# The order of GpSimd's mask and of the loads in the recurrence of a linear-attention and mixture-of-experts kernel

## The chip, the cores and the metric

The kernel runs on one core of one Trainium2 chip. The metric is device time in microseconds (us); six runs of the kernel before gave a median of 430.74 us, between 429.99 and 431.18. Engines are written as in the profile: PE is TensorE, PEld its weight loads, DVE is VectorE, ACT is ScalarE, POOL is GpSimd, SP is the sync engine, which here issues the DMAs.

## The reference

Two blocks follow one another. The first is a gated recurrence over time with one state of 48 x 48 for each of 4 x 8 heads:

```
state = np.zeros((B, H, D, D))            # B, H, S, D = 4, 8, 768, 48
for t in range(S):
    state = alpha[:, :, t, :, None] * state + einsum('bhd,bhe->bhde', k[:, :, t], v[:, :, t])
    y[:, :, t] = einsum('bhd,bhde->bhe', q[:, :, t], state)
```

Its output, as 3072 rows of 384, goes to a mixture of eight experts. Each row goes to the expert with the highest logit, and its result is scaled by that expert's softmax weight:

```
logits = x @ w_gate                       # (3072, 384) @ (384, 8)
expert_idx = argmax(logits)               # gate_w: its softmax probability
h = maximum(x[rows of e] @ w1[e], 0)      # w1[e]: 384 x 1024
y[rows of e] = h @ w2[e]                  # w2[e]: 1024 x 384
out = gate_w[:, None] * y
```

All inputs and the output are float32.

## The kernel before

**Chunks and pairs.** Time is cut into 24 chunks of 128 steps (six chunks for each of four batches). A chunk holds all eight heads. The main loop (L696) takes two chunks at a time, s = 2, 4, ..., 20, but the stages are staggered over several chunks: a pair works on the results of chunks s and s+1, the scores of s+2 and s+3, the transposes of s+3 and s+4, and the elementwise work of s+5 and s+6. The schedule is manual: the order of the calls in the text is the order of the instructions on each engine, and each engine executes its own in that order.

**One chunk.** `logs` (L324): ACT takes the logarithm of alpha. `cums` (L334): PE sums it over time with a triangular matrix into one PSUM bank named `cum`, of which there is one, and ACT makes two exponentials of it, `icp` (exp of the negative) and `cp`. `operands` (L356): POOL multiplies k by icp (L360) and q by cp (L362) into the tile kqb. `transposes` (L364): PE turns kqb by heads, ACT copies kT and DVE copies qT out of PSUM. `scores` (L376): PE multiplies kT and qT into sA and sB; DVE masks sA to dA; ACT copies sB to dB (L388), and POOL then zeroes the part of dB above the diagonal with an affine_select (L389). `weighs` (L420): PE multiplies dA and dB with v into y (L426). `reads` (L402): PE adds the query times the state U of the chunk before (L414). `products` and `state` (L440, L458): PE forms k times v, ACT or DVE takes it out of PSUM, POOL adds the old state and scales by the decay E. `rows`, `keep_rows`, `store_rows`: PE turns the results and forms the gate's logits, and SP stores 128 rows of x to DRAM.

**Ranks.** Every fourth chunk, `choose` (L489) picks the expert of each row on DVE, and POOL adds up the choices in `ohs` (L500). In the pair after, `rank_products` (L502) multiplies them on PE (L505, L506), behind the first `cums` of that pair, which gives each row its place in its expert's list.

**Loads.** alpha (a), k, q and v of a chunk are 192 KB each. `to_load` (L314) is one list of loads in the order of their issue; `more_loads(n)` (L320) issues the next n of it. Each pair issues 2, 2 and 5 of them, and SP's other DMAs stand between: `decay_out` after the first two, `store_rows(s-1)` after the second two, `decay_in` and `store_rows(s)` after the five. All are on SP's one queue. The tiles of a, k and q have five buffers each, v has six, so a load waits until the chunk five (or six) before is done with its buffer.

**The order on POOL in a pair** is: the state of s+1, the mask of dB for s+2, `operands(s+5)`, the state of s+2, small copies of logits for s and s+1, `operands(s+6)`, the mask of dB for s+3, some constants (`late_consts`, L176, iotas and casts in the first pairs), and the adds of ohs every second pair. On ACT it is: the copy of PSUM for the state, the logarithm of s+5, the copy of dB for s+2, the logarithm of s+6, the exponentials of s+5, the copy of kT for s+3, the copy of rows, the exponentials of s+6, kT for s+4, rows, and the copy of dB for s+3.

After the loop come the last two chunks and the routing (to about 152 us), then the eight experts with two layers of matmuls each (L968, L984), the gathers of rows and the stores of results by indirect DMAs on POOL.

Of the kernel before, what the change touches and what calls it, by code (L numbers as in the profile page):

```python
# [18 lines left out]
def kernel(  # L19
# [267 lines left out]
    with tc.tile_pool(name="ld", bufs=6) as ld, \  # L287
# [21 lines left out]
        def some_loads(names):  # L309
# [3 lines left out]

        to_load = [  # L314
            (n, x + d) for x in range(7, NT + 2)
            for n, d in ((("a", 1), ("k", 0), ("q", 0), ("v", -2)) * 2)[3 * (x > 7) :][:4]
        ]


        def more_loads(n):  # L320
            for _ in range(min(n, len(to_load))):
                load(*to_load.pop(0))
# [53 lines left out]
        def scores(s):  # L376
            d = st[s]
            sA = ps.tile([C, NP, C], F32, name="sA")
            sB = ps.tile([C, NP, C], F32, name="sB")
            for p in range(NP):  # L380
                for t, r in ((sA, 0), (sB, DP)):
                    nc.tensor.matmul(  # L382
                        t[:, p, :], lhsT=d["kT"][r : r + D, p, :], rhs=d["qT"][r : r + D, p, :], start=True, stop=True,
                    )
            d["dA"] = work.tile([C, NP, C], F32, name="dA")
            nc.vector.tensor_tensor(d["dA"][:], sA[:], cmask[:, None, :].to_broadcast([C, NP, C]), op=ALU.mult)
            d["dB"] = work.tile([C, NP, C], F32, name="dB")
            nc.scalar.copy(d["dB"][:], sB[:])  # L388
            nc.gpsimd.affine_select(  # L389
                d["dB"][:], d["dB"][:], compare_op=ALU.is_ge, fill=0.0,  # L390
                base=0, pattern=[[0, NP], [1, C]], channel_multiplier=-1,
            )
# [3 lines left out]
        def results_of(s):  # L396
            y = [ps.tile([C, 2, NP // 2, C], F32, name=f"y{h}") for h in range(2)]
            for i in range(2):
                st[s + i]["y"] = [t[:, i] for t in y]
            return y  # L400

        def reads(s, first=None):  # L402

            d = st[s]
            if s % NB == 0:
                return
            if first is None:
                first = s % 2 == 0 or s % NB == 1
            for n in range(NP // 2):
                for h in range(2):  # L410
                    p = n + h * (NP // 2)
                    for a in range(2):
                        r = a * DP
                        nc.tensor.matmul(  # L414
                            d["y"][h][at(p, a) : at(p, a) + DP, n, :],
                            lhsT=st[s - 1]["U"][r : r + D, p, :], rhs=d["qT"][r : r + D, p, :],
                            start=(n == 0 and first), stop=False, skip_group_check=True,
                        )

        def weighs(s, h, first=False):  # L420

            d = st[s]
            for n in range(NP // 2):
                p = n + h * (NP // 2)
                for a in range(2):
                    nc.tensor.matmul(  # L426
                        d["y"][h][at(p, a) : at(p, a) + DP, n, :],
                        lhsT=d["v"][:, 2 * p + a, :], rhs=d["d" + "AB"[a]][:, p, :],
                        start=(first and n == 0), stop=True, skip_group_check=True,
                    )  # L430

        def results_to(s, y, h):
            if h == 0:
                yT = work.tile([C, 2, 2, NP // 2, C], F32, name="yT", bufs=1)
                for i in range(2):
                    st[s + i]["yT"] = yT[:, :, i]
                st[s]["yTs"] = yT
            nc.vector.tensor_copy(st[s]["yTs"][:, h], y[h][:])

        def products(s):  # L440

            d = st[s]
            if s >= NT or s % NB + 1 == NB:
                return
            kv = ps.tile([C, NP, C], F32, name="s" + "BA"[s % 2])[:, :, :D]
            for p in range(NP):
                for i, r in enumerate((0, DP)):
                    nc.tensor.matmul(  # L448
                        kv[r : r + DP, p, :], lhsT=kqb[s % 4][:, 0, 2 * p + i, :], rhs=d["v"][:, 2 * p + i, :D],
                        start=True, stop=True,  # L450
                    )
            d["acc"] = work.tile([C, NP, D], F32, name="acc" + "BA"[s % 2], bufs=1)
            if s % 2:
                nc.vector.tensor_tensor(d["acc"][:], kv, st[s - 1]["U"][:, :, :D], op=ALU.add)
            else:
                nc.scalar.copy(d["acc"][:], kv)

        def state(s):  # L458
            d = st[s]
            if s >= NT or s % NB + 1 == NB:  # L460
                return
            if s % 2 == 0 and s % NB:
                nc.gpsimd.tensor_tensor(d["acc"][:], d["acc"][:], st[s - 1]["U"][:, :, :D], op=ALU.add)
            d["U"] = Ub[s % len(Ub)]
            nc.gpsimd.tensor_tensor(
                d["U"][:, :, :D], d["acc"][:], d["E"].unsqueeze(2).to_broadcast([C, NP, D]), op=ALU.mult,
            )
# [17 lines left out]
        def store_rows(s):  # L485
            r0 = s * C + (s >= NT // 2)
            nc.sync.dma_start(x_d[r0 : r0 + C, :], st[s]["xs"][:])
# [115 lines left out]
        def do(f, i, *a):  # L603
            if 0 <= i < NT:
                f(i, *a)
# [90 lines left out]
        for s in range(2, NT - 2, 2):  # L696
            more_loads(2)
            if s == 2:
                store_rows(0)
            do(decay_out, s + 4)  # L700
            more_loads(2)

            for _ in range(8 if s > NT - 8 else 0):
                next(parts, None)
            y = results_of(s)
            reads(s)
            reads(s + 1)

            weighs(s, 0)
            weighs(s, 1)  # L710
            products(s + 1)
            products(s + 2)
            weighs(s + 1, 0)
            results_to(s, y, 0)
            weighs(s + 1, 1)
            results_to(s, y, 1)
            state(s + 1)
            do(logs, s + 5)
            if hots:
                one_hots(hots.pop(0))  # L720
            scores(s + 2)
            do(logs, s + 6)
            do(cums, s + 5)
            ranks = y[0][:].rearrange("r i p t -> r (i p t)")
            ranked = [rank_products(g, ranks[:, : len(g) * E]) for g in groups_of if g[-1] == s - 1]
            counts = ranks[:, C : C + E]
            if s in (TE, ORD):

                nc.tensor.matmul(
                    counts, lhsT=ones_sq[:], rhs=ohs[:, s, :], start=True, stop=True, skip_group_check=True,  # L730
                )
            if s == ORD:
                early_slots(ranks[:, 2 * C : 2 * C + EB * NQ])
                fetch_lot(0)
            for r in ranked if s < ORD else ():
                slots_of(*r)
            transposes(s + 3)
            do(operands, s + 5)
            state(s + 2)
            rows(s)  # L740
            keep_rows(s)
            store_rows(s - 1)
            if s == ORD:
                for r in ranked:
                    slots_of(*r)
                key = standing(counts[0:1, :])
                one_hots(hots.pop(0))
                one_hots(hots.pop(0))
                route = rps.tile([C, Dm], F32, name="cum")
                tokens_of_slots(0, TE)  # L750
            do(cums, s + 6)
            do(transposes, s + 4)
            more_loads(5)
            do(decay_in, s + 4)
            rows(s + 1)
            keep_rows(s + 1)
            do(operands, s + 6)
            if s == TE:
                close_early(counts[0:1, 0:1])
            scores(s + 3)  # L760
            store_rows(s)
            if s == 2:

                nc.sync.dma_start(x_d[N // 2 : N // 2 + 1, :], zero_w[:])
            late_consts(s + 2)
            late_consts(s + 3)
            if s == ORD:
                choose(groups_of[-2])
            if hots:
                one_hots(hots.pop(0))  # L770
            for g in groups_of[:-2]:
                if g[-1] == s + 1:
                    choose(g)
            for _ in range(4 if s == NT - 8 else 0):
                next(parts, None)
# [25 lines left out]
        s = NT - 2  # L801
# [329 lines left out]
```

## Time and profile before

| | |
|---|---|
| median of six runs | 430.74 us (429.99 to 431.18) |
| the profiled execution | 432.11 us, span 430.2 us |
| PE busy | 421.1 us, 98% of the span |
| DVE, ACT, POOL busy | 140.6, 108.3, 140.3 us |
| mean granted PE clock | 0.994 |
| loop (pairs s = 2 to 20) | from 28.99 to 139.74 us |
| DMA | 59.43 MB, most of it in the first 140 us at about 200 GB/s; 114614 of 132576 packets under 512 B |

All times below are microseconds from the start of the span of this one execution. A line of an engine's order of time gives the start, the duration, the engine, the source line, the operation, the output and its inputs, and in brackets the idle time before it and what ended it. A line of the waits names who waited for whom: the total, how often, and the longest. The chain of work that ended last gives start and duration of each piece. A line with `SPq` is the issue of a DMA by the sync engine, not its transfer. The clock of PE is a share of full speed, as granted.

### The profile page before, as it was taken

What the parts mean: (1) busy time and instruction counts of PE and PEld (TensorE: products, weight loads), DVE (VectorE), ACT (ScalarE), POOL (GpSimd) and SP (SyncE); (2) the same over time, 40 slices, a digit from 0 to 9 for tenths busy, and PEclk for the clock granted to TensorE, in tenths of its full rate; (3) what the DMA queues carried; (4) which work ended last, traced back from release to release, by engine and by line L of the source; (5) the groups of instructions that cost most, each with busy time, mean ns of one, the idle gap of its engine ahead of it and who ended that gap; (6) DMA issues with size and microseconds to landing.
All of it is one profiled execution on the core that took longest, in us unless ns stands there. A gap on an engine that the chain in (4) does not pass through costs nothing.

```text
span 430.2 us, 7708 instructions
## 1 busy us (share of the span) xinstructions
PE 421.1 (98%) x2990; PEld 285.4 (66%) x2990; DVE 140.6 (33%) x414; ACT 108.3 (25%) x230; POOL 140.3 (33%) x254
## 2 busy tenths in 40 slices
PE   8999899999999999999999999999999999999995
PEld 6888788888889887555555555655655455565452
DVE  6434457575768834711012101201201101111100
ACT  4565455555542321111111111011111110011011
POOL 4395677576665150160160110024010010010011
PEclk9999899999999999999999999999999999999999
DMA  9999999999977242994542610724620050000000
GB/s 161 180 164 205 202 204 201 192 193 194 182 197 215 83 114 91 395 400 161 179 129 70 250 38 2 270 74 114 224 105 18 2 183 20 0 32 20 1 33 30
DMA packets 132576, 59.43 MB, mean 138 GB/s; under 512 B 114614, under 2 KB 127452, under 8 KB 132538
## 3 DMA queue, kind: packets, MB, share of 16 engines
q1 hardware_dynamic: 127720, 48.96, 45.1%
q0 software_dynamic: 3328, 9.94, 7.0%
q8 instruction: 24, 0.39, 0.4%
q10 hardware_dynamic: 1490, 0.02, 0.2%
q14 instruction: 14, 0.11, 0.1%
HBM read 49.32 MB, written 9.98 MB: 138 GB/s over the span
## 4 chain that ended last, share of the span: by engine, by line
PE 62%; issue 28%; POOL 5%; DMA 2%; SPq 1%; DVE 1%; POOLq 0%; ACT 0%; DVEq 0%
PE zp L984 16%; PE hp L968 14%; PE sA L382 5%; PE y L426 5%; PE tp L369 4%; PE xr L474 4%; PE cum L337 3%; POOL out_dram L990 3%; PE y L414 2%; PE xr L612 2%; PE xtp L960 1%; PE sB L448 1%; POOL xg L269 1%; PE hp L785 1%; DMA k_sb<-in_k_dram 1%
## 5 line engine op out<-in xcount | busy, mean ns | idle before, releaser
L984 PE MATMUL zp<-w,h_sb 128*128 128x384 f32 (+2 forms) x560 | 137.1, 487 | 0.0
L968 PE MATMUL hp<-xT,w 128*128 128x416 f32 (+3 forms) x384 | 125.1, 486 | 0.0
L984 PEld LDWEIGHTS zp<-w,h_sb 128*128 128x128 f32 (+2 forms) x560 | 73.6, 163 | 56.3 <-issue 14.8
L968 PEld LDWEIGHTS hp<-xT,w 128*128 128x128 f32 x384 | 71.8, 190 | 51.9 <-issue 37.8
L990 POOL DMA_INDIRECT out_dram<-zo,o_idx x26 | 25.8, 992 | 219.2 <-ACT zo L989 214.3
L973 DVE TENSOR_SCALAR h_sb<-hp 128x416 f32<-128x416 f32 (+3 forms) x32 | 17.8, 557 | 149.3 <-PE hp L968 149.3
L989 ACT ACTIVATE zo<-zp,gw 128x384 f32<-128x384 f32 x26 | 15.1, 580 | 123.7 <-PE zp L984 119.1
L975 ACT ACTIVATE h_sb<-hp 128x416 f32<-128x416 f32 (+3 forms) x32 | 15.7, 490 | 107.3 <-PE hp L968 107.3
L269 POOL DMA_INDIRECT xg<-x_rows,g_idx x26 | 25.1, 965 | 11.1 <-issue 6.4
L382 PE MATMUL sA<-qT,kT 48*128 48x128 f32 x192 | 28.2, 288 | 0.2 <-DVE qT L372 0.2
L382 PE MATMUL sB<-qT,kT 48*128 48x128 f32 x192 | 28.3, 288 | 0.0
L962 DVE COPY xT<-xtp 128x384 f32<-128x384 f32 (+3 forms) x29 | 13.0, 484 | 44.4 <-PE xtp L960 44.3
L426 PE MATMUL y<-dB,vb 128*64 128x128 f32 x192 | 25.3, 278 | 1.7 <-POOL dB L389 1.7
L360 POOL TENSOR_TENSOR kqb<-k_sb,icp 128x384 f32<-128x384 f32 x23 | 23.0, 1000 | 11.8 <-ACT icp L340 8.8
L382 PEld LDWEIGHTS sA<-qT,kT 48*128 48x128 f32 x192 | 23.6, 190 | 4.7 <-issue 2.1
L426 PE MATMUL y<-dA,vb 128*64 128x128 f32 x192 | 26.3, 277 | 0.0
L369 PE MATMUL tp<-ident,kqb 128*128 128x128 f32 x192 | 25.7, 277 | 0.2 <-POOL kqb L362 0.2
L369 PEld LDWEIGHTS tp<-ident,kqb 128*128 128x128 f32 x192 | 22.2, 143 | 5.3 <-issue 2.7
L474 PE MATMUL xr<-back,yT 128*128 128x104 f32 x192 | 25.1, 274 | 0.0
L474 PEld LDWEIGHTS xr<-back,yT 128*128 128x128 f32 x192 | 23.6, 192 | 0.8 <-ACT xs L481 0.2
L382 PEld LDWEIGHTS sB<-qT,kT 48*128 48x128 f32 x192 | 23.6, 190 | 0.0
L372 DVE COPY qT<-tp 128x512 f32<-128x512 f32 x24 | 16.5, 689 | 20.2 <-PE tp L369 20.1
(178 smaller groups left out, 436.9 us busy)
## 6 DMA issues: line engine op xcount, KB each, us to landing
w<-in_moe_w_dram SPq DMA_DIRECT2D x14, 1536.0 KB, 7.0
x_rows<-xs SPq DMA_DIRECT2D x24, 196.0 KB, 3.9
a_sb<-in_alpha_dram SPq DMA_DIRECT2D x24, 192.0 KB, 4.1
k_sb<-in_k_dram SPq DMA_DIRECT2D x24, 192.0 KB, 3.8
q_sb<-in_q_dram SPq DMA_DIRECT2D x24, 192.0 KB, 4.4
vb<-in_v_dram SPq DMA_DIRECT2D x24, 192.0 KB, 3.5
w<-in_moe_w_dram SPq DMA_DIRECT2D x12, 128.0 KB, 3.7
w<-in_moe_w_dram SPq DMA_DIRECT2D x8, 192.0 KB, 4.3
```

Source lines behind the costliest of these rows:

```text
L269: nc.gpsimd.indirect_dma_start(out=xg[:, j, :], out_offset=None, in_=x_d[: N + 1 if n else TE * C + 1, :], in_offset=bass.IndirectOffsetOn ...
L360: k.tensor_tensor(kq[:, 0, :, :D], d["k"][:], heads(d["icp"]), op=ALU.mult)
L369: nc.tensor.transpose(tp[:, p, :], pair(kqb[s % 4][:, i], p), ident[:])
L372: nc.vector.tensor_copy(d[n][:], tp[:])
L382: nc.tensor.matmul(t[:, p, :], lhsT=d["kT"][r : r + D, p, :], rhs=d["qT"][r : r + D, p, :], start=True, stop=True,)
L426: nc.tensor.matmul(d["y"][h][at(p, a) : at(p, a) + DP, n, :], lhsT=d["v"][:, 2 * p + a, :], rhs=d["d" + "AB"[a]][:, p, :], start=(first an ...
L474: nc.tensor.matmul(xr[:, p, :], lhsT=d["yT"][:, p // (NP // 2), p % (NP // 2), :], rhs=back[:, p, :], start=True, stop=True)
L968: nc.tensor.matmul(hp[:, c0:c1], lhsT=w1[:, a, f * C : (f + 1) * C], rhs=xT[:, a, c0:c1], start=(a == 0), stop=(a == DB - 1),)
L973: nc.vector.tensor_relu(h[:, f, c0:c1], hp[:, c0:c1])
L975: nc.scalar.activation(h[:, f, c0:c1], hp[:, c0:c1], AF.Relu)
L984: nc.tensor.matmul(zp[i * wd : (i + 1) * wd, :], lhsT=h[:, f, c : c + wd], rhs=w2[:, f, :], start=(f == 0), stop=(f == FB - 1), skip_group ...
L990: ins = nc.gpsimd.indirect_dma_start(out=out[:, :], out_offset=bass.IndirectOffsetOnAxis(ap=idx, axis=0), in_=zo[:], in_offset=None, bound ...
```

## The change

Two edits, both inside the recurrence. In every pair, `operands(s+6)` is issued after `scores(s+3)` in place of before it. Of the engines, only POOL has instructions of both: the mask of dB for chunk s+3 now stands ahead of the two multiplies of chunk s+6. (For s = TE = 16 the two small DVE instructions of `close_early` stay ahead of the scores.) In the pairs s = 18 and 20 there is no chunk s+6.

And the list of loads has another order from chunk 8 on. Before, the groups from x = 8 on were v(x-2), a(x+1), k(x), q(x); now they are k(x), v(x-2), a(x+1), q(x). The group of x = 7 (a8, k7, q7, v5) stays. The number of loads issued at each place stays.

```
         to_load = [
             (n, x + d) for x in range(7, NT + 2)
-            for n, d in ((("a", 1), ("k", 0), ("q", 0), ("v", -2)) * 2)[3 * (x > 7) :][:4]
+            for n, d in (
+                (("a", 1), ("k", 0), ("q", 0), ("v", -2)) if x == 7 else (("k", 0), ("v", -2), ("a", 1), ("q", 0))
+            )
         ]
...
             rows(s + 1)
             keep_rows(s + 1)
-            do(operands, s + 6)
             if s == TE:
                 close_early(counts[0:1, 0:1])
             scores(s + 3)
+            do(operands, s + 6)
             store_rows(s)
```

## The prediction

> **What bounds the kernel now.** The page first: TensorE (PE) is busy for nearly the whole span, so only PE's idle time and PE's slow time can be won.
>
> ```profile
> PE 421.1 (98%) x2990; PEld 285.4 (66%) x2990; DVE 140.6 (33%) x414; ACT 108.3 (25%) x230; POOL 140.3 (33%) x254
> ```
>
> Next, the view of who waited for whom, cut to PE. One wait stands out: the matmuls of `weighs` (L426) for the mask of dB that GpSimd (POOL) makes at L389. The weight loads of the same place add up to 1.96 us.
>
> ```profile
> PE y L426 <- POOL dB L389: 1.7, 1, 1.7
> ```
>
> Then the chain of work that ended last, around that wait. It names the cause: the load of k for chunk 8 lands 3.88 us after its issue, POOL's `operands(8)` waits for it, and the mask of chunk 5 stands behind both multiplies.
>
> ```profile
> 37.89 3.88 DMA k_sb<-in_k_dram
> ...
> 41.90 0.82 POOL kqb L360
> ...
> 42.86 0.99 POOL kqb L362
> 43.85 0.60 POOL dB L389
> ...
> 44.50 1.09 PE y L426 x14
> ```
>
> POOL's own order of time shows that it had nothing to do for 1.92 us before it:
>
> ```profile
> 39.66 0.32 POOL L482 COPY xs<-lgn 128x8 f32<-128x8 f32 x2
> 41.90 1.00 POOL L360 TENSOR_TENSOR kqb<-k_sb,icp 128x384 f32<-128x384 f32 x1 [1.92 <-DMA k_sb<-in_k_dram]
> ```
>
> Last, PE's busy time and granted clock in four neighbouring stretches of about 3.4 us (columns: length, busy, clock, DMA share, GB/s):
>
> ```profile
> 40.00:42.57 2.57, 2.57 (x68) 1.00 1.20 214
> 42.57:45.99 3.42, 1.71 (x24) 1.00 0.90 177
> 45.99:49.40 3.41, 3.41 (x22) 0.50 1.12 242
> 49.40:52.80 3.40, 3.40 (x29) 1.00 1.16 215
> ```
>
> The half-idle stretch is followed by 3.41 us at half clock, which costs 3.41/2 = 1.7 us. Elsewhere in the loop the clock reads 1.00. So the wait costs 2.08 us (42.42, where the next matmul was due, to 44.50) plus 1.7, about 3.8 us. The loop's pairs agree: the reads (L414) of pair s=4 start at 39.98 and those of s=6 at 54.46, 14.48 us, while pair s=10 (76.22 to 86.80), with the same matmuls but for two small ranking ones, takes 10.58.
>
> The DMA share is near 1 from 30 to 108 us: the sync queue (SP) is paced by its transfers, 0.4 to 1.1 us from one load's issue to the next.
>
> **The change, part by part.**
>
> *The mask moves ahead of `operands(s+6)`*, in eight pairs (s=2 to 16); nothing is added or removed. dB of chunk 5 is copied by ScalarE (ACT) from 40.12 to 40.71, so the mask (0.64) runs about 40.78 to 41.42, a microsecond before PE needs it at 42.42. The wait goes whatever k does: 2.08 us and the 1.7 of slow clock behind it, -3.8.
>
> The two multiplies (2 x 1.0) now wait for the score matmuls and ACT's copy. In a plain pair that is from 64.42 to about 66.5 (dB's copy of 65.20 plus 0.59, plus the mask), so they end 1.4 us later than the 67.0 of before. Behind them on POOL stand the late constants, the four adds of ohs (L500), the state Ub and the next mask. Constants 0.7 and adds 1.03 then end at 70.2, Ub at 70.7, and the next mask runs at 70.76 as before. Who waits: PE's ranking matmuls at 70.87 (0.7 us of cover), the reads of Ub at 76.22 (5.5 us), the transposes of chunk 12 after 73 (5 us). Cost zero; with the cover gone, up to 1.4 us in each of eight pairs. The tiles of k and q come free 1.4 us later, for loads five chunks on: not felt.
>
> In pair s=4, PE itself comes 2.1 us earlier, so the adds of ohs are tight. The multiplies of chunk 8 start at 41.4, the second by 42.86 at the latest (there q had landed in the trace); constants take 1.36 (44.40 to 45.76), the third add ends 0.77 later: 45.4 to 45.95. PE's ranking matmul is due at 45.3. A new wait of 0.2 to 0.7 us.
>
> *The order of loads.* Before: v6 a9 k8 q8 v7 | a10 k9 | q9 v8 | a11 k10 ... After: k8 v6 a9 q8 k9 | v7 a10 | q9 k10 | v8 a11 ... A bar is where SP's other issues (decay rows, x rows) stand; they keep their places. All loads have one size, so each takes over the slot that stood at its place. k comes two slots earlier, v and alpha one slot later, q stays. k8 goes from 37.89 to 36.71 and lands about 40.5, before POOL can use it at 41.4. v6 goes to 37.15 and lands by 41.45 at the longest v time on record (4.3), and PE uses it at 41.93; a9 lands by 42.6 (longest 4.7), used at 42.87. Both are covered, by 0.3 to 0.5 us; gone, that much is paid.
>
> What is late next is alpha of chunk 10. SP's own order of time:
>
> ```profile
> 42.74 0.38 SPq L307 DMA_DIRECT2D a_sb<-in_alpha_dram  x1
> 43.16 1.06 SPq L307 DMA_DIRECT2D k_sb<-in_k_dram  x1
> ```
>
> a10 leaves its slot to v7 and is issued at 43.16. In ACT's order of time its logarithm started at 47.74, right after dB, without a wait:
>
> ```profile
> 47.26 0.58 ACT L388 COPY dB<-sB 128x512 f32<-128x512 f32 x1 [3.87 <-PE sB L382]
> 47.74 0.53 ACT L326 ACTIVATE ln<-a_sb 128x384 f32<-128x384 f32 x1
> ```
>
> With the stall gone, scores(6) start at 45.51 - 2.08 = 43.43. Pair s=2 shows the steps at full clock (scores at 32.79): the logarithm follows after 1.72, the second cumulative sum `cums` of the pair after 3.59. So the logarithm wants a10 at 45.15 and PE wants to start cums(10) at 47.08. ACT is in order: queued behind the logarithm are both exponentials of cums(9), 1.28 us from its start to their end in pair s=2 (34.51 to 35.79), and cums(10) needs their PSUM bank back. If a10 lands at L, PE starts cums(10) at L + 1.28 + 0.1 (a hand-over): a stall of L - 45.7. Measured landings near here are 3.3 us (k11) to 4.1 (median of alpha); k8 took 3.88. L is 46.46 to 47.26, the stall 0.8 to 1.6. I take 3.85, near k8's row at the same load: 1.3 us. The wait for ohs lies inside this stall, since PE then waits for cums(10) anyway. The bounds by all rows: 3.1 (shortest alpha) gives 0.6, 4.7 gives 2.2.
>
> Later loads: a12 takes k11's slot at 53.32 and lands about 57.4; its logarithm, at 59.54 before, is wanted at 57.0: 0.4 late, inside the 0.6 us that PE leaves between the first exponentials and the second sum. From a13 on alpha has 5 us and more. q9 (44.75 + 4.3 = 49.1) is wanted by POOL at 49.1; q12 63.3 against 63.6.
>
> *The clock after the new stall* is the unknown. A stretch that was half idle (1.71 of 3.42) was followed by half clock; the 0.42 us PE wait at 148.5 was not. 1.3 of 3.4 is 38%: bounds 0 and 1.7 us. I take 0, since a stretch must hold half its length idle in the only row that throttled.
>
> The Trainium skill ("TensorE: Matmul & The Clock Gate", sections "Part 1" and "Why this matters for your kernels") says the same of the window, 3.4 us and free-running, but lets the clock fall only after a gap of about 3 us or a whole idle window. Here 1.9 us sufficed, so the measurement decides; by the page's rule a 1.3 us stall is certainly safe, which is the same sum.
>
> **Sum.** -3.8 + 1.3 + 0 = -2.5 us, off the profiled execution's 432.11 (430.2 span and 1.9 around it): 429.6. That execution lies 1.37 above the median 430.74; the same difference gives 428.2. After the loop PE hands the gain on: its waits from 140 to 166 us add up to about 0.7 us, and the expert stage is one run of matmuls.
>
> **The rivals.** A change of 0.2% (0.86 us) is about what a measurement can tell from none.
>
> No second stall: a10 lands sooner since SP's backlog is small there (DMA share 0.69 at 43 to 44 us). It would have to land in 2.5 us, under the shortest row of 3.1. Then the ohs wait of about 0.45 shows instead: -3.35, 427.4.
>
> The half clock does not come off: either the new stall throttles too (-2.5 + 1.7), or the half clock was this profiled execution's alone (it is the slowest of the seven times) and the timed ones pay only the 2.08 (-2.08 + 1.3). Both give about -0.8: 429.9. For it: one execution shows the half clock, and no row shows it twice. Against: the six times spread over 1.2 us, less than one half clock, so most of them pay the same.
>
> Nothing changes, 430.7: POOL's or SP's stall moves to another place of equal size. Against it: no other load in the loop keeps its own reader waiting over 0.4 us.
>
> Slower: a10 waits behind a deeper queue than any row shows. Stall plus half clock equal what was won when L - 45.7 + 1.7 = 3.8, at L = 47.8, a landing of 4.64 us, and the time is measurably worse from 5.5 us on; 6 us gives a stall of 3.45: +1.35, 432.1. For it: the DMA share is 1.12 from 46 us. Against: the longest row is 4.7.
>
> **How the numbers follow.** The forecast 0.42 (own range 427.6 to 428.9), no second stall 0.15, half clock stays 0.20, nothing 0.08, slower 0.15. 428.2 is predicted. Leaving out the slower case and the best part of the second gives 427.0 to 431.0. Faster by over 0.2%: 0.42 + 0.15 + half of 0.20 = 0.67; same 0.10 + 0.07 = 0.17; slower 0.16.
>
> **What would show it.** The wait of L426 for POOL's dB is gone and pair s=4 takes about 12 us. Right: ACT's logarithm of chunk 10 waits 1 to 2 us for alpha, and PE waits at L337 for ACT. The ranking matmul (L505) may wait for ohs. The clock stays at 1.00 to 60 us. Wrong: a clock of 0.50 near 50 us, a wait for v6 at L448, or PE waits at L505 in later pairs, which would say that POOL's new order has a price.

## The result, and the profile after

The changed kernel takes 432.22 us (median of 23 runs, 431.44 to 433.93) against 430.91 us (48 runs, 429.99 to 432.42): 1.0032 times before, with a 95% interval of 1.0024 to 1.0039. It is 1.3 us slower; the forecast was 428.2, 2.5 us faster. The profiled execution took 432.28 us with a span of 430.6.

The first reading is as forecast. TensorE's waits in the changed kernel hold no wait for GpSimd's mask any more (columns: who waited for whom, us in total, times, longest; the lines left out lie outside the loop):

```profile
...
PE sA L384 <- DVE accA L456: 1.1, 2, 0.8
PE cum L339 <- ACT cpb L343: 0.6, 1, 0.6
...
PE tp L371 <- DVE qT L374: 0.4, 1, 0.4
...
```

(Lines have moved by two: L384 is the scores, L456 the state's sum on VectorE, L339 and L343 the cumulative sum and its exponential, L371 and L374 the transposes and their copy.) The second line is the forecast wait for alpha of chunk 10. The first and the third are not in the forecast: TensorE waits for VectorE.

The span divides well by pairs of chunks. Each entry is the time from the first read matmul (L414, L416 after) of a pair to that of the next, in us. Pairs with the same matmuls agree within 0.03 us wherever TensorE waits for nothing.

| kernel | s=4 | s=8 | s=12 | s=16 |
|---|---|---|---|---|
| before, the profile of the forecast | 14.41 | 11.13 | 10.70 | 10.70 |
| changed | 11.71 | 11.60 | 11.52 | 11.51 |
| difference | -2.70 | +0.47 | +0.82 | +0.81 |

So, between these two profiles, 2.7 us were won in one pair and 2.1 lost in three. The spans differ the other way by 0.4 us, since the changed kernel's profile also begins slower: its first matmuls take longer (the first two cumulative sums 1.49 us in place of 0.81). In the 14 profiles of this study the first read of pair s=2 lies between 28.8 and 30.0 us (28.92 and 29.97 here). This does not follow the edits: a kernel that is the one before up to there has 29.99 (the idle multiplies below). It is taken as chance here, and leaves -2.70 + 2.10 = -0.6 where the runs measure +1.3. Half of the question is thus what made three pairs longer, the other half why pair s=4 gained so little in the runs.

The three pairs first. Here are VectorE and then GpSimd around the end of pair s=6, in the changed kernel, in order of time (start, duration, instruction):

```profile
64.85 0.17 DVE L494 TENSOR_REDUCE lmin<-lgn 128x4 f32<-128x32 f32 x1
65.05 0.81 DVE L496 TENSOR_TENSOR sc<-lgn,lmin 128x32 f32<-128x32 f32 x1
65.90 0.93 DVE L497 TENSOR_TENSOR sc<-sc,first_w 128x32 f32<-128x32 f32 x1
66.86 0.19 DVE L499 TENSOR_REDUCE top<-sc 128x4 f32<-128x32 f32 x1
...
67.30 0.34 DVE L456 TENSOR_TENSOR accA<-sA,Ub 128x192 f32<-128x192 f32 x1
```

```profile
64.17 0.68 POOL L391 TENSOR_SCALAR_AFFINE_SELECT dB<-dB 128x512 f32<-128x512 f32 x1 [1.34 <-ACT dB L390]
64.82 0.99 POOL L362 TENSOR_TENSOR kqb<-k_sb,icp 128x384 f32<-128x384 f32 x1
65.78 1.00 POOL L364 TENSOR_TENSOR kqb<-q_sb,cpb 128x384 f32<-128x384 f32 x1
```

The same two instructions of the choice of experts in the kernel before, when GpSimd's multiplies (64.42 to 66.38) and its mask (66.33 to 66.96) were over:

```profile
66.97 0.17 DVE L492 TENSOR_REDUCE lmin<-lgn 128x4 f32<-128x32 f32 x1
67.17 0.19 DVE L494 TENSOR_TENSOR sc<-lgn,lmin 128x32 f32<-128x32 f32 x1
67.40 0.19 DVE L495 TENSOR_TENSOR sc<-sc,first_w 128x32 f32<-128x32 f32 x1
```

Two instructions of 0.19 us took 0.81 and 0.93. Each began inside a multiply of GpSimd and ended with it: 65.86 against 65.81, and 66.83 against 66.78. The reduction (0.17) passed beside the same multiply. Before, VectorE was held at this place too, but other instructions were, and the choice came after them: the one-hots, 0.28 and 0.34 us alone, met the second multiply and the mask.

```profile
65.72 0.75 DVE L575 TENSOR_SCALAR oh_r<-iota_r,rc 128x129 f16<-128x129 f32 x1
66.38 0.67 DVE L576 TENSOR_SCALAR oh_c<-iota_h,rc,tokv 128x129 f16<-128x129 f32 x1
```

From the pair's first read, the choice's last instruction ended 3.0 us on before (68.03) and 4.0 us on in the changed kernel (67.37). In the pairs s=8 and 12 the order of VectorE puts the state's sum accA behind the choice, and the next scores need the PSUM bank that accA reads:

```profile
67.70 0.37 PE L384 MATMUL sA<-qT,kT 48*128 48x128 f32 x1 [0.39 <-DVE accA L456]
```

In pair s=16 there is no accA, and the way to TensorE is longer. All of VectorE runs about 0.7 us later behind the choice, so the shift L519 (0.17 us alone) meets the first of the next two multiplies (114.24 to 115.24) and the cast L524 the second (115.20 to 116.20); before, the cast had met the first. The change did not move these two multiplies. The copy of qT stands behind them, and TensorE's transposes wait for it (the third line of the waits):

```profile
114.63 0.63 DVE L519 TENSOR_SCALAR rc_i<-slot_i 128x4 int32<-128x4 int32 x1
...
115.37 0.85 DVE L524 CAST rc<-rc_i 128x8 f32<-128x8 int32 x1
```

```profile
116.87 0.66 PE L371 MATMUL tp<-ident,kqb 128*128 128x128 f32 x4 [0.37 <-DVE qT L374]
```

Theory A says, then: two of VectorE's instructions, and all behind them, are held by GpSimd's multiplies, which the change moved to the place of the choice. Rivals: B, the order of the loads loses (alpha and v come a slot later); C, GpSimd's own results come late, and TensorE waits for them.

### The profile page after: what moved, and what is told of

Read it like the earlier page. It is cut to its first block, busy times and chain, and to the rows that moved or that the text cites. A ratio compares the mean times of both kernels' runs of the same rounds, so it can differ in the third digit from the quotient of the medians.

```text
span 430.6 us, 7694 instructions
## 1 busy us (share of the span) xinstructions
PE 421.1 (98%) x2990; PEld 284.8 (66%) x2990; DVE 142.3 (33%) x414; ACT 108.2 (25%) x230; POOL 141.1 (33%) x254
## 4 chain that ended last, share of the span: by engine, by line
PE 60%; issue 28%; POOL 4%; DVE 4%; DMA 2%; ACT 1%; POOLq 0%; DVEq 0%; SPq 0%; ACTq 0%
PE zp L986 16%; PE hp L970 14%; PE sA L384 5%; PE xr L476 4%; PE tp L371 4%; PE y L428 4%; PE cum L339 3%; POOL out_dram L992 3%; PE y L416 2%; PE xr L614 2%; PE xtp L962 1%; POOL xg L269 1%; DMA a_sb<-in_alpha_dram 1%; PE hp L787 1%; PE sB L450 1%
## 5 line engine op out<-in xcount | busy, mean ns | idle before, releaser
L384 PE MATMUL sA<-qT,kT 48*128 48x128 f32 x192 | 27.7, 284 | 1.4 <-DVE accA L456 1.1
L384 PE MATMUL sB<-qT,kT 48*128 48x128 f32 x192 | 27.7, 285 | 0.0
L384 PEld LDWEIGHTS sA<-qT,kT 48*128 48x128 f32 x192 | 23.1, 187 | 6.0 <-issue 1.9
L371 PE MATMUL tp<-ident,kqb 128*128 128x128 f32 x192 | 25.5, 274 | 0.6 <-DVE qT L374 0.4
L371 PEld LDWEIGHTS tp<-ident,kqb 128*128 128x128 f32 x192 | 21.8, 141 | 5.8 <-issue 2.4
L374 DVE COPY qT<-tp 128x512 f32<-128x512 f32 x24 | 16.6, 690 | 20.7 <-PE tp L371 20.6
L391 POOL TENSOR_SCALAR_AFFINE_SELECT dB<-dB 128x512 f32<-128x512 f32 x24 | 15.9, 664 | 22.4 <-ACT dB L390 20.9
```

The source lines that it names most:

```text
L371: nc.tensor.transpose(tp[:, p, :], pair(kqb[s % 4][:, i], p), ident[:])
L374: nc.vector.tensor_copy(d[n][:], tp[:])
L384: nc.tensor.matmul(t[:, p, :], lhsT=d["kT"][r : r + D, p, :], rhs=d["qT"][r : r + D, p, :], start=True, stop=True,)
L391: nc.gpsimd.affine_select(d["dB"][:], d["dB"][:], compare_op=ALU.is_ge, fill=0.0, base=0, pattern=[[0, NP], [1, C]], channel_multiplier=-1,)
```

## The experiments

The experiments ran in three groups, each on one chip and with its own runs of the kernel before. Before's medians differ between the groups (430.15 to 431.94), so times are compared within a group.

**One half of the change each.** The mask first, with the loads as before:

```
-            do(operands, s + 6)
             if s == TE:
                 close_early(counts[0:1, 0:1])
             scores(s + 3)
+            do(operands, s + 6)
```

> The order of loads is that of before; only GpSimd's mask stands ahead of the second operands in every pair. Theory A: the loss is VectorE's: the two tensor_tensor of the choice of experts (L494, L495 of before, 0.19 us each there) read and write SBUF beside GpSimd's multiplies and are held until those end. Then both last 0.8 to 0.95 us in the pairs s=6, 10 and 14, the pairs s=8, 12 and 16 take about 11.6, 11.5 and 11.5 us as in the changed kernel (11.13, 10.70, 10.70 before), and the time is 0.5 to 1.3 us above before. Theory B: the loss comes from alpha and v being loaded a slot later; then these pairs take what they took before, pair s=4 loses its 2 us wait, and the time is 1 to 2 us below before.

The loads alone:

```
-            for n, d in ((("a", 1), ("k", 0), ("q", 0), ("v", -2)) * 2)[3 * (x > 7) :][:4]
+            for n, d in (
+                (("a", 1), ("k", 0), ("q", 0), ("v", -2)) if x == 7 else (("k", 0), ("v", -2), ("a", 1), ("q", 0))
+            )
```

> Only the order of loads is changed; GpSimd's mask stands behind the second operands as before. Theory A: the choice's tensor_tensor last 0.19 us again and the pairs s=8, 12 and 16 take 11.13, 10.70 and 10.70; k of chunk 8 is there about 1.2 us sooner, so PE's wait for the mask in pair s=4 falls from 2.0 to about 0.7 us, and the time is 0.7 to 1.5 us below before. Theory B: the time is 1 us or more above before, with waits for alpha on ScalarE in many pairs.

| | time, us | before, us | ratio (95%) | s=4 | s=8 | s=12 | s=16 |
|---|---|---|---|---|---|---|---|
| mask only | 432.01 | 431.94 | 1.0003 (0.9991 to 1.0015) | 11.31 | 11.60 | 11.52 | 11.51 |
| loads only | 432.06 | 431.94 | 1.0011 (0.9998 to 1.0023) | 12.86 | 11.14 | 11.53 | 10.70 |

The long pairs belong to the mask's new place: theory B's account of them falls. The time of the first, though, missed its expectation (0.5 to 1.3 us above): it is no higher than before's on this chip, although its profile lost another 0.81 us in pair s=2, behind a late alpha. The second missed its own: pair s=4 still waits. GpSimd's order of time in the loads-only kernel shows why:

```profile
40.37 1.00 POOL L362 TENSOR_TENSOR kqb<-k_sb,icp 128x384 f32<-128x384 f32 x1
43.51 1.00 POOL L364 TENSOR_TENSOR kqb<-q_sb,cpb 128x384 f32<-128x384 f32 x1 [2.14 <-DMA q_sb<-in_q_dram]
44.46 0.64 POOL L391 TENSOR_SCALAR_AFFINE_SELECT dB<-dB 128x512 f32<-128x512 f32 x1
```

k was there at once; q, which kept its slot and also stands ahead of the mask, was not. The wait passed from one load to the other. Pair s=12 took 11.53 with the mask at its old place and without a wait of TensorE for GpSimd there, a first sign that VectorE's hold has other places too.

**The changed kernel with the old order where a choice is made**, at s = 6, 10 and 14:

```
+            if not (s % 4 != 2 or s == 2):
+                do(operands, s + 6)
             if s == TE:
                 close_early(counts[0:1, 0:1])
             scores(s + 3)
-            do(operands, s + 6)
+            if s % 4 != 2 or s == 2:
+                do(operands, s + 6)
```

> The changed kernel, but in the pairs s=6, 10 and 14, whose end holds a choice of experts, the second operands stand ahead of the mask again. Theory A: all that was lost comes back there, the pairs s=8, 12 and 16 take 11.13, 10.70 and 10.70, pair s=4 stays at about 11.7, and the time is 2.1 us below the changed kernel, about 1 us below before. Theory B: 432.2 as the changed kernel.

**The mask first in pair s=2 alone, and alpha earlier** in the list of loads:

```
-            do(operands, s + 6)
+            if not (s == 2):
+                do(operands, s + 6)
...
             scores(s + 3)
+            if s == 2:
+                do(operands, s + 6)
...
+            for n, d in (
+                (("a", 1), ("k", 0), ("q", 0), ("v", -2)) if x == 7 else
+                (("k", 0), ("a", 1), ("v", -2), ("q", 0)) if x == 8 else (("a", 1), ("k", 0), ("v", -2), ("q", 0))
+            )
```

> The mask stands first in pair s=2 alone, and the loads from chunk 8 on go k8 a9 v6 q8, a10 k9 v7 q9, a11 k10 v8 q10 and so on. Theory A, with the wait for alpha of chunk 10 gone (it lands near 43.5 us, wanted at 45.2): what is left in pair s=4 is PE's wait of 0.5 us for the adds of the choices, the pair takes about 11.1 us, the others what they take before; 1.3 to 1.7 us below before, about 429.4. Theory B: alpha early alone accounts for it, and e3 stays at 432.

In the group of the two halves, beside before's 431.94: the first took 431.12 us, 0.9987 (0.9967 to 1.0006), the second 431.00 us, 0.9988 (0.9973 to 1.0004). Both lie below before, by less than was expected, and neither interval excludes no change. Their pairs s=8 and 12 were 11.14 and 10.70 in both, as theory A expects, and s=16 was 10.70 in the second. But the first's s=4 took 12.68 (its alpha of chunk 10 came 2.4 us late, and the adds 0.9), its s=16 took 11.26; the second's s=4 took 10.90, its s=6 11.74 and its s=14 11.49 (10.6 and 11.05 elsewhere). The strays of the later pairs can be read. In the second, q of chunk 10 was late in a pair with the old order, and the mask waited behind it as in before:

```profile
53.52 1.00 POOL L365 TENSOR_TENSOR kqb<-q_sb,cpb 128x384 f32<-128x384 f32 x1 [1.07 <-DMA q_sb<-in_q_dram]
54.47 0.64 POOL L392 TENSOR_SCALAR_AFFINE_SELECT dB<-dB 128x512 f32<-128x512 f32 x1
```

In its pair s=14 and in the first's s=16, GpSimd itself was late: it had waited 2.81 and 3.47 us for a decay row (Eb), worked on without a pause, and came late to the mask behind its multiplies. TensorE's weight loads waited 0.17 and 0.37 us for that mask. From the first kernel:

```profile
102.77 0.51 POOL L467 TENSOR_TENSOR Ub<-accA,Eb 128x192 f32<-128x192 f32 x1 [3.47 <-DMA Eb<-decay_rows]
```

```profile
109.74 0.13 PEld L428 LDWEIGHTS y<-dB,vb 128*64 128x64 f32 x1 [0.37 <-POOL dB L391]
```

So these losses are the old order's, in which the mask stands behind the multiplies, and not VectorE's. VectorE was held there as well, but at its one-hots. From the second kernel, for the one-hots at the end of pair s=12's text, which run as the reads of s=14 begin:

```profile
96.50 1.06 DVE L578 TENSOR_SCALAR oh_r<-iota_r,rc 128x129 f16<-128x129 f32 x1
97.48 1.05 DVE L579 TENSOR_SCALAR oh_c<-iota_h,rc,tokv 128x129 f16<-128x129 f32 x1
```

beside GpSimd's multiplies of 96.48 to 97.48 and 97.43 to 98.43. Small shifts decide which VectorE instruction meets which multiply.

**The choice moved out of the multiplies' way.** In the changed kernel, the choice stands ahead of the scores in place of behind them, so that VectorE makes it while GpSimd waits for ScalarE's copy. GpSimd's multiplies are no earlier:

```
+            for g in groups_of[:-2]:
+                if g[-1] == s + 1:
+                    choose(g)
             if s == TE:
                 close_early(counts[0:1, 0:1])
             scores(s + 3)
             do(operands, s + 6)
...
-            for g in groups_of[:-2]:
-                if g[-1] == s + 1:
-                    choose(g)
```

> The changed kernel with one move: the choice of experts, with its adds, stands ahead of the scores of s+3 in place of behind them, so that VectorE makes it while GpSimd waits for the mask, and not beside the second operands. GpSimd's multiplies end no sooner than in the changed kernel. Theory A (VectorE held by GpSimd's multiplies): the two tensor_tensor of the choice last 0.19 us, the pairs s=8, 12 and 16 take 11.1, 10.7 and 10.7 us, and PE's wait for the adds in pair s=4 goes too; 1.5 to 2.5 us below the changed kernel. Theory C (GpSimd's late multiplies themselves are what PE waits for in these pairs): the pairs stay at 11.5 to 11.6 and the time within 0.7 us of the changed kernel.

It ran beside the changed kernel:

> The changed kernel once more, beside the next three on the same chip. The pairs s=8, 12 and 16 take about 11.6, 11.5 and 11.5 us; its median is 0.2 to 0.4% above before. Should it be within 0.1%, the loss depends on the chip.

and with the loads in the order k8 a9 v6 q8, then a10 k9 v7 q9 and so on (the list of the alpha-early kernel above):

> As the one before, with the loads from chunk 8 on in the order k8 a9 v6 q8, a10 k9 v7 q9, a11 k10 v8 q10 and so on. Theory A: no wait is left in pair s=4, it takes 10.7 to 10.9 us, and the whole lies 0.5 to 1.1 us below the one before and 1.5 to 2.2 us below before: the fastest of all. Theory C: 431 to 432 on a chip where before takes 431.

| | time, us | ratio to before (430.55 us) | s=4 | s=8 | s=12 | s=16 |
|---|---|---|---|---|---|---|
| changed, again | 431.72 | 1.0026 (1.0014 to 1.0039) | 11.73 | 11.61 | 11.51 | 11.51 |
| choice early | 429.39 | 0.9979 (0.9967 to 0.9992) | 11.44 | 11.14 | 10.71 | 10.70 |
| and alpha early | 428.56 | 0.9949 (0.9929 to 0.9969) | 10.67 | 11.14 | 10.71 | 10.70 |

This settles the three pairs. In the choice-early kernel, VectorE's two instructions are back at 0.19, and TensorE's waits for accA and qT are gone, though GpSimd's multiplies run as late as in the changed kernel (64.82 and 65.78 there; counted from the first read of pair s=8, 2.0 us in place of 1.45):

```profile
62.28 0.19 DVE L496 TENSOR_TENSOR sc<-lgn,lmin 128x32 f32<-128x32 f32 x1
62.50 0.19 DVE L497 TENSOR_TENSOR sc<-sc,first_w 128x32 f32<-128x32 f32 x1
```

```profile
64.83 1.00 POOL L362 TENSOR_TENSOR kqb<-k_sb,icp 128x384 f32<-128x384 f32 x1
65.78 1.00 POOL L364 TENSOR_TENSOR kqb<-q_sb,cpb 128x384 f32<-128x384 f32 x1
```

Theory C falls: with the multiplies no earlier, the three pairs are as short as before's. The move is worth 431.72 - 429.39 = 2.3 us; the three pairs account for 0.47 + 0.80 + 0.81 = 2.1, and pair s=4, where TensorE's wait for the adds went, for 0.3. Alpha a slot or two sooner takes pair s=4 from 11.44 to 10.67, where no wait is left in it. This last kernel (six runs) is the fastest of all, 0.5% below before.

**The cost put into the kernel before**, with nothing moved:

```
             scores(s + 3)
+            if s in (6, 10, 14):
+                for _ in range(3):
+                    nc.gpsimd.tensor_tensor(still[:], still[:], still[:], op=ALU.mult)
```

> The kernel before, with nothing moved, but in the pairs s=6, 10 and 14 GpSimd multiplies a tile of zeros with itself three times (0.67 us each, 2 us in all) behind the mask, just where VectorE makes the choice; nothing reads the result. Theory A: the choice's tensor_tensor last 0.6 to 0.7 us each, and the pairs s=8, 12 and 16 take 0.3 to 0.8 us longer than 11.13, 10.70 and 10.70, 1 to 2 us in all above before. Theory C: GpSimd has room for 2 us, and the time stays within 0.5 us of before.

The time fits, 431.62 against 430.55, 1.0026 (1.0010 to 1.0042), but the profile does not: only the first of the two instructions was held, and the pairs took 11.14, 10.99 and 10.70.

```profile
65.14 0.42 DVE L494 TENSOR_TENSOR sc<-lgn,lmin 128x32 f32<-128x32 f32 x1
65.59 0.19 DVE L495 TENSOR_TENSOR sc<-sc,first_w 128x32 f32<-128x32 f32 x1
```

```profile
64.89 2.06 POOL L763 TENSOR_TENSOR still<-still 128x256 f32<-128x256 f32 x3
```

The first ends at 65.56, just after the first idle multiply (64.89 to 65.51). The second starts at 65.59, together with the next idle multiply, and is not held. The profiled execution's span is 428.4, and the 12 runs' median span is 429.85, so what the median run paid is not shown, and this experiment is inconclusive on the price.

**How long before waits in pair s=4.** The kernel before, profiled twice more, with both halves beside it again:

> The kernel before, profiled once more. If the profile of before that the forecast was made from is typical, pair s=4 takes 12.7 us (a wait of about 2 us for GpSimd's mask) and, where the stretch at half clock follows, 14.4. If that profile was an outlier, the pair takes 10.9 to 12 us at full clock; the landing of k and q of chunk 8, 3.9 us after their issue or sooner, decides it. The other pairs take 11.13 (s=8), 10.70 (s=12) and 10.70 (s=16).

> As the one before, once more: 12.7 or 14.4 us for pair s=4 if the first profile is typical, 10.9 to 12 if it was an outlier.

> The mask first and the loads as before, again, on the chip of the next one. If the loss is VectorE's at the choice, the pairs s=8, 12 and 16 take 11.6, 11.5 and 11.5 us, and the time is 0.1 to 0.3% above before wherever before's pair s=4 has the shorter wait. If the order of the loads is what loses, the time is at least 0.2% below before.

> The loads in the new order and the mask behind the second operands, again. If k's earlier load only hands the wait to q (which keeps its slot and stands ahead of the mask too), pair s=4 takes 11 to 13 us as in before and the time is within 0.2% of before. If the order of the loads is what loses, it is 0.2% or more above.

| | time, us | ratio to before (430.15 us) | s=4 | s=8 | s=12 | s=16 |
|---|---|---|---|---|---|---|
| before, second profile | 430.87 | one run | 11.86 | 11.14 | 11.54 | 10.70 |
| before, third profile | 430.71 | one run | 12.24 | 11.15 | 11.53 | 10.70 |
| mask only, again | 431.48 | 1.0028 (1.0016 to 1.0040) | 11.13 | 11.61 | 11.62 | 11.51 |
| loads only, again | 430.39 | 1.0020 (1.0002 to 1.0039) | 12.23 | 11.14 | 10.70 | 10.70 |

The first profile of before was an outlier in pair s=4, for its stretch at half clock above all; the third profile's 12.24 lies between the two expectations, near the longer wait at full clock. TensorE's wait for the mask in the second profile (its weight loads waited 1.0):

```profile
PE y L426 <- POOL dB L389: 0.8, 1, 0.8
```

and 1.1 (weight loads 1.4) in the third, with the clock at 1.00 behind both. Before's runs bear that out: the first profile's mean clock was 0.994, and among 85 runs of before with a clock on record only 7 read 0.993 or 0.994, six of them on the chip of the first two halves. The idle-multiply kernel, which is before up to there, took 11.32. And before has a hold of its own in pair s=12: in the second profile, VectorE's shift of four integers by L517, 0.17 us alone, ran into the multiply of 90.71 to 91.71,

```profile
90.79 0.95 DVE L517 TENSOR_SCALAR rc_i<-slot_i 128x4 int32<-128x4 int32 x1
```

and TensorE waited 0.4 us for the copy of qT behind it, as in the changed kernel's pair s=16. The third profile has the same (0.93 and 0.4).

The mask alone loses 0.28% on this chip and nothing measurable on that of the first two halves, where before itself was 1.8 us slower; why the chips differ is not shown. The loads alone are near no change on both (0.11% and 0.20%, the second interval reaching down to 0.02%; two of its 12 runs, 433.8 us at a mean clock of 0.991, weigh in it).

## Why the prediction was wrong

**The mask's move "cost zero".** This step failed. The prediction followed GpSimd's instructions to those who wait for their results, and found cover of 0.7 us and more; that cover held, and no wait of TensorE for GpSimd's results came up in pairs s=8, 12 and 16. It did not ask who works beside them. The 1.4 us is also too small for the multiplies themselves: it counts from the end of the mask that stood behind them (67.0), while they had ended at 66.38. From the pair's first read, their end moved by 2.0 us (1.37 to 3.41). This put them beside the choice of experts on VectorE at the ends of s=6, 10 and 14: +0.47, +0.82 and +0.81 in the pairs that follow, 2.1 us in all against the first profile of before. Against its second and third, whose pair s=12 is as long, it is +0.46, 0 and +0.81, about 1.3. (At the end of s=2 the choice was held as well, and TensorE had other waits there.) The trace of before had the sign: the one-hots shown above, and the cast L522, beside GpSimd's multiply of 49.38, against the same cast while GpSimd ran no multiply but an indirect DMA (137.55 to 138.50):

```profile
49.59 0.86 DVE L522 CAST rc<-rc_i 128x8 f32<-128x8 int32 x1
```

```profile
137.56 0.19 DVE L522 CAST rc<-rc_i 128x8 f32<-128x8 int32 x1
```

The Trainium skill has the rule ("SBUF — State Buffer", section "SBUF: two separate sides"): GpSimd and VectorE share a pair of SBUF ports, which goes for a whole instruction to the one that starts first, against VectorE's instructions with two SBUF inputs and those in a two-port mode. The rows agree: the choice's two instructions with two SBUF inputs (0.19 us, then 0.81 and 0.93), the cast (0.19, then 0.86) and the one-hots (0.28 and 0.34, then 1.06 and 1.05) were held to the end of GpSimd's instruction, the reduction (0.17) was not. Whether the cast and the one-hots ran in a two-port mode, no run here shows. The rule gives no price, but it points at this change, and the prediction did not weigh it.

**"-3.8".** The mechanism was right, the size was the first profile's own. The wait of 2.08 us with 1.7 us of half clock behind it was forecast to go, and it went; but two further profiles of before lost 11.86 - 10.67 = 1.2 and 1.6 us there (10.67 is the pair with no wait left, in the kernel with the choice and alpha early), with no half clock. The rival "the half clock does not come off" named this chance (half clock in the profiled execution alone) and gave it 0.20, together with a second way to the same time. (The 14.48 us that it reads for pair s=4 are 14.41 by the first reads' rows.)

**The wait for alpha of chunk 10, 1.3 us.** Right in place; that the size fits is in part luck. ScalarE's order of time in the changed kernel:

```profile
45.66 0.59 ACT L390 COPY dB<-sB 128x512 f32<-128x512 f32 x1 [1.21 <-PE sB L384]
47.72 0.52 ACT L328 ACTIVATE ln<-a_sb 128x384 f32<-128x384 f32 x1 [1.48 <-DMA a_sb<-in_alpha_dram]
```

Its load, issued at 43.38, took 4.25 us (3.85 was assumed) and landed 0.6 us later than forecast, at 47.63. From there the sum held: 47.63 + 1.28 + 0.1 = 49.01, and cums(10) began at 49.05. But TensorE itself came 1.05 us later in this profile than in the one of the forecast, and without that the stall would have been longer. TensorE's weight loads lost 0.47 us at the ranking matmuls (the profile names no releaser; the third of the adds of ohs ends there) and 0.72 at cums(10): 1.2 us, and pair s=4 took 11.71 ("about 12"). The forecast that the ohs wait lies inside held too.

**k two slots earlier.** "Lands about 40.5": it was there at 40.37 in the loads-only kernel. The prediction credited the end of the wait to the mask's move and not to k, and the two halves show that: k alone handed it on to q.

**The clock after the new stall, 0.** Right: 1.00 throughout in the changed kernel.

**Later loads.** a12 was forecast 0.4 us late without a cost: ScalarE waited 0.37 for it, and pair s=6 took 10.64.

Put together by the profiles: the changed kernel's four pairs sum to 46.34 and 46.36 us, before's to 45.24 and 45.62 in its second and third profile, a loss of 0.7 to 1.1 us; the runs measure 1.3 and 1.2. The profiles are of different chips, and what makes up the rest is open. A slower kernel had a chance of 0.16 in the forecast, but by another mechanism (a deeper DMA queue): here alpha of chunk 10 took 4.25 us, below the longest row of 4.7.

## What to carry to other kernels

Before moving work on GpSimd, list what VectorE executes at the new place, instruction by instruction, as well as who waits for the result: a short VectorE instruction can wait for the whole of a long GpSimd one, and everything behind it on VectorE waits too. Put VectorE's short chains where GpSimd waits for something else; here that was worth 2.3 us against the changed kernel, and 0.2% against the one before. And a stall that hangs on when a DMA lands should be sized from several executions, above all when its price includes a stretch at half clock.

## What the runs showed of the hardware that was not expected

- A held VectorE instruction waited only for the GpSimd instruction that was running: at two idle multiplies of 0.62 and 0.67 us, 0.08 us apart, the next one got in (0.42, then 0.19 us), while the kernel's own multiplies of 1.0 us, whose rows overlap by 0.03 us, caught both (0.81 and 0.93).
- Which VectorE instruction is caught changes between executions of one kernel, and TensorE's loss with it: pair s=12 of the kernel before took 10.70, 11.54 and 11.53 us in three profiles.
- Outside the span, the executions of the kernels with the mask first in every pair spent 1.72 to 1.79 us, those of before 1.95 (medians). The mask's place is not the reason: the kernel with the idle multiplies, in which nothing is moved, spent 1.76. Nothing in the traces explains the 0.2 us, and it was not pursued.
